# A hand-written instruction order replaced by another: units 8 to 11 moved forward, fewer and finer loads, more placed warm-up matmuls, three scheduled steps pinned

## The chip, the cores and the metric

The kernel runs on one core of a Trainium2 chip. The time is that of one execution on the device in microseconds (us). Engines are named as in the profile: PE (matrix engine), PEld (its weight loads), DVE (vector), ACT (scalar), POOL (GpSimd) and SP, which issues the DMAs.

## The reference, cut to what matters

Two parts follow each other. A decaying recurrence over 4 batches, 8 heads, 768 tokens, head width 32 and state width 16, in chunks of 32 tokens, gives 3072 tokens of 256 numbers. A feed-forward layer with softplus takes them to 2048 and back to 256.

```
log_a = log(clip(a, 1e-6, 1))
for each chunk c:                       # 32 tokens
    cum = cumsum(log_a[c]);  L = causal * exp(cum_i - cum_j)
    y[c]  = (C B^T * L) x  +  (C state) * exp(cum)
    state = exp(sum(log_a[c])) * state + sum_j B_j x_j exp(cum_last - cum_j)
x = y as [3072, 256]
h = x @ w_in;   g = softplus(h);   out = g @ w_out      # [256 -> 2048 -> 256]
```

All values are 32-bit; w_in and w_out arrive as 64-bit numbers. A matmul of full precision in the feed-forward part is made of three fast ones, from a high and a low part of each factor.

## The kernel before, in words

**Units.** The recurrence is cut into 24 units of 128 tokens with all 8 heads; units 0 to 5 are batch 0, and so on. A unit needs: its data (`un`, for units 0 to 3 together with `hc`), a mask of decays built by POOL (`D`), B scaled by decay (`B`) and C scaled by decay (`C`), scores (`S`, PE), the scores times the mask (`M`, two DVE instructions, tile `m`), the new state (`U`, PE and DVE, tiles `zp` and `state`), the previous state spread out (`T`, tile `tb`), the read of the state (`R`, PE) and the sum within the unit (`I`, PE, tile `yp`), the product with the growth factors (`G`, tile `y` on DVE, then `xh` on ACT) and the low part of the result (`X`, tile `xl`). From unit 8 on, units go in pairs: `v` (PE and the states) and `e` (read, state, growth, high and low part).

**Growth factors.** For units 0 to 2 they are made on the chip (`gb`, `gq`). For the others the logs are summed by rows (`growth`), stored to DRAM (`gd`) and read back, spread over 32 partitions per head (`gg`, two loads for 2 or 3 units; the pool holds two such tiles). `loga` and `logr` take the logs of the two layouts of `a`; `ft` and `fr` make the factors by token and by row from them and from the constants `kc` and `kb`.

**Weights.** `w` loads a piece of 64-bit weights (even numbers: w_in, odd: w_out, each for two of the 16 blocks of 128 hidden columns; four raw tiles). `W`, called six times, turns it into a high and a low part: ACT, DVE, DVE, DVE, ACT, DVE.

**Feed-forward steps.** Tokens are cut into six groups of 512 (units 0 to 3 are group 0). `Fj.k` is the first product of group j and block k (six matmuls, tile `hp`), `Hk` the half of `F0.k` for units 0 and 1, `Pj.k` the three steps softplus (ACT, tile `e`), high part (ACT, `gh`) and low part (DVE, `gl`), and `Zj.k` the second product (six matmuls into the accumulators `acc`). Groups 0 and 1 go through blocks 0 to 7 first and through 8 to 15 later; `K`, `L` and `E0` take the accumulators out.

**What sets the order.** Up to `E0` the order of the whole program is the list `ORDER`, word for word, on every engine (`in_order[0]` is True, and each engine is a queue in order). `warmN` places N matmuls without use of their result. From step 28 on a loop over steps takes over: `begin` (F and its parts), `values` (Z), and `fills`: `split_unit`, `attend_scores`, `prefetch`, pairs. There `in_order[0]` is False: PE and the DMAs keep the program's order, while a planner places the work of DVE, ACT and POOL, also between words of `ORDER`. In the profile, what was placed in order has line 127 (L127), the free instructions have their own lines, such as L254, L255, L368 and L384. DMAs have line 137.

Of the kernel before, what the change touches and what calls it, by code (L numbers as in the profile page):

```python
# [50 lines left out]


ORDER = """
zero warm8 la kc kb hc0 w0 loga un0 loga w2 gb hc1 fr0 w4 ft0 fr0 un2 lr hc3 hc2 un6 W0 S0 w6 ft0 W0 un1 W0 un5 D1 B0
un4 W2 un7 fr0 un3 gq0 fr0 D0 W0 ft2 gq0 M0 w5 W0 logr M0 gq2 logr ft2 growth D2 I0 gq2 B2 growth S2 gd G0 U2 W0 G0 S1
M2 W4 X0 fr2 M2 C1 U0 B1 D3 M1 U1 C2 warm3 U0 M1 T1 S3 D4 U1 fr2 U2 T2 R1 S4 B4 T3 B6 W4 W2 R2 C3 B3 I1 W2 W4 C4 I2 G1
gg3 M3 G1 R3 X1 gg10 U3 C5 M3 warm1 M4 I3 D8 U3 M4 fr2 U6 G2 fr2 D7 U4 G3 G2 H0 U6 G3 U4 X2 S7 X3 T4 W2 F0.0 M7 W2 w1
H1 W4 P0.0 R4 W2 P0.0 w3 F0.1 M7 C7 H2 P0.0 D5 P0.1 I4 T7 W6 F0.2 P0.1 un10 W4 H3 W6 P0.2 P0.1 R7 P0.2 W4 F0.3 B7 W1
P0.2 H4 P0.3 G4 I7 W1 G4 B10 P0.3 W6 F0.4 X4 H5 P0.3 P0.4 W1 U7 F0.5 T5 un11 U7 W1 S5 P0.5 T8 w7 W1 W6 S6 M5 W6 w10 W1
R5 W6 W3 Z0.0 M5 W5 W3 D6 I5 W5 P0.4 F0.6 un8 W3 Z0.1 G5 P0.6 W3 gg6 G5 M6 W3 F0.7 w9 X5 P0.6 W3 B8 W7 C8 Z0.2 M6 W7  # L60
D9 G7 I6 W5 G7 P0.5 Z0.3 un9 X7 G6 S11 P0.5 G6 gg8 X6 P0.7 P0.4 F1.0 P0.7 W5 C9 W5 w15 P0.7 S9 P1.0 W5 B9 W9 W7 Z0.4
P0.6 W9 F1.1 W7 P1.0 W9 W7 w8 P1.0 Z0.5 P1.1 W9 W7 W9 w12 F1.2 M9 P1.1 W10 W9 Z0.6 P1.2 P1.1 W8 W10 M9 F1.3 P1.2 W8
D10 W10 Z0.7 P1.3 W8 F1.4 L0 K0 P1.3 W8 Z1.0 P1.3 P1.4 w13 W8 W10 F1.5 W8 W10 w14 P1.2 P1.4 W15 W10 Z1.1 P1.5 P1.4 W13
W15 F1.6 W15 P1.5 W13 P1.5 Z1.2 P1.6 W13 W15 F1.7 W13 P1.6 w11 W15 P1.6 W13 Z1.3 W15 P1.7 W13 W14 F0.8 W12 W14 P1.7
W14 W12 Z1.4 P0.8 P1.7 W12 F0.9 W14 P0.8 W12 W14 P0.8 Z1.5 W12 W14 P0.9 W12 W11 F0.10 P0.9 W11 W11 Z1.6 P0.10 P0.9 W11
F0.11 P0.10 W11 P0.10 Z1.7 W11 P0.11 F0.12 P0.11 K1 P0.11 L1 S8 P0.12 Z0.8 M8 M8 F0.13 P0.12 D11 P0.12 Z0.9 P0.13
F0.14 P0.13 P0.13 Z0.10 P0.14 F0.15 P0.14 P0.14 Z0.11 P0.15 F1.8 P0.15 P0.15 Z0.12 P1.8 v8 P1.8 P1.8 Z0.13 M11 un13
C10 v8 un12 S10 M11 e8 e8 M10 Z0.14 e8 M10 e8 gg12 F1.9 C11 e8 v10 P1.9 P1.9 P1.9 F1.10 v10 e10 P1.10 F1.11 e10 e10
P1.10 e10 P1.10 Z0.15 P1.11 e10 P1.11 P1.11 E0
"""  # L70
# [31 lines left out]


@with_exitstack
def recurrence_then_ffn(ctx: ExitStack, tc: tile.TileContext, fst, un, at, al, w_in, w_out, const, outT):
# [29 lines left out]
    def load(out, in_):  # L135

        tc.keep_in_program_order(nc.sync.dma_start(out, in_))  # L137
# [107 lines left out]
    def split_unit(i):  # L245
        if i < FIRST:
            return
        t = bc_s[i]
        b_rows = p2.tile([P, NQ, P], F32R, tag="b_rows", name=f"b_rows{i}")

        def split(out, j):
            raw = t[:, j * NQ * P : (j + 1) * NQ * P].rearrange("p (q t) -> p q t", q=NQ)
# [1 line left out]
            A.activation(out, raw, AF.Copy, scale=be)  # L254
            V.scalar_tensor_tensor(out, raw, g, out.bitcast(F32), op0=ALU.mult, op1=ALU.add)  # L255
# [678 lines left out]
```

## Time and profile before

| | |
|---|---|
| time, 3 runs | 348.7 us median (347.05 to 349.23) |
| the profiled execution | 347.7 us, its span 345.7 us |
| mean granted clock of PE | 0.975 |
| PE busy | 329.7 us, 95% of the span |
| DVE, ACT, POOL busy | 205.2, 170.9, 37.8 us |
| moved by DMA | 34.99 MB |

A row of the timeline reads: start, duration, engine, line, operation, output<-input, shapes, how many were merged, and in brackets the idle time before and what ended it. A row of the table by windows reads: the window and its length, then busy time and number of instructions of PE, PEld, DVE, ACT and POOL (an engine with none is left out), the granted clock of PE, the busy share of the 16 DMA engines, and GB/s. PE's end times are modelled, so the distance from one start to the next says more than the duration.

### The profile page before, as it was taken

What the parts mean: (1) busy time and instruction counts of PE and PEld (TensorE: products, weight loads), DVE (VectorE), ACT (ScalarE), POOL (GpSimd) and SP (SyncE); (2) the same over time, 40 slices, a digit from 0 to 9 for tenths busy, and PEclk for the clock granted to TensorE, in tenths of its full rate; (3) what the DMA queues carried; (4) which work ended last, traced back from release to release, by engine and by line L of the source; (5) the groups of instructions that cost most, each with busy time, mean ns of one, the idle gap of its engine ahead of it and who ended that gap; (6) DMA issues with size and microseconds to landing.
All of it is one profiled execution on the core that took longest, in us unless ns stands there. A gap on an engine that the chain in (4) does not pass through costs nothing.

```text
span 345.7 us, 5174 instructions
## 1 busy us (share of the span) xinstructions
PE 329.7 (95%) x1972; PEld 258.5 (75%) x1972; DVE 205.2 (59%) x358; ACT 170.9 (49%) x309; POOL 37.8 (11%) x32
## 2 busy tenths in 40 slices
PE   8588999999999879999999999999999999999996
PEld 4335877588878557888888878888888888888885
DVE  0985797999952882666673775677575243222222
ACT  3642863778744252454462572465553443454451
POOL 1432104020010110110110110110110000000000
PEclk9896799999999989999999999999999999999999
DMA  7972547545000504623512514513420100010001
GB/s 241 396 298 70 158 149 248 161 124 174 0 2 0 183 33 124 210 56 128 154 30 93 137 55 145 151 33 111 134 91 12 21 0 2 1 61 2 0 0 61
DMA packets 21895, 34.99 MB, mean 101 GB/s; under 512 B 1648, under 2 KB 11120, under 8 KB 21872
## 3 DMA queue, kind: packets, MB, share of 16 engines
q1 hardware_dynamic: 21872, 34.68, 31.8%
q8 instruction: 15, 0.25, 0.3%
q14 instruction: 8, 0.07, 0.1%
HBM read 28.29 MB, written 3.24 MB: 91 GB/s over the span
## 4 chain that ended last, share of the span: by engine, by line
PE 69%; DMA 13%; DVE 9%; ACT 4%; issue 2%; SPq 2%; ACTq 0%; DVEq 0%
PE acc L127 33%; PE hp L127 31%; DMA gg<-gd 4%; DMA bc<-in_un 3%; DMA gd<-lr 3%; PE yp L127 3%; PE sp L127 2%; DVE w L127 2%; SPq L137 2%; DMA wraw<-in_w_in 1%; DMA un<-in_un 1%; DVE m L127 1%; DMA un<-in_fst 1%; DVE gl L127 1%; ACT e L666 1%
## 5 line engine op out<-in xcount | busy, mean ns | idle before, releaser
L678 DVE TENSOR_TENSOR gl<-e,gh 128x512 fp32r<-128x512 f32 x68 | 54.1, 799 | 52.3 <-ACT gh L672 52.0
L127 PE MATMUL hp<-xh,wih 128*128 128x512 f32 (+1 forms) x204 | 79.1, 388 | 0.3 <-ACT xh L127 0.3
L127 PE MATMUL hp<-xh,wil 128*128 128x512 f32 (+1 forms) x204 | 78.1, 383 | 0.0
L127 PE MATMUL hp<-xl,wih 128*128 128x512 f32 (+1 forms) x204 | 78.1, 383 | 0.0
L127 PE MATMUL acc<-gh,woh 128*128 128x512 f32 x188 | 75.7, 402 | 1.0 <-DVE half L127 0.8
L666 ACT ACTIVATE e<-hp 128x512 f32<-128x512 f32 x68 | 40.5, 595 | 68.6 <-PE hp L127 68.3
L127 PE MATMUL acc<-gl,woh 128*128 128x512 f32 x188 | 73.7, 392 | 0.0
L127 PE MATMUL acc<-gh,wol 128*128 128x512 f32 x188 | 73.6, 391 | 0.0
L127 PEld LDWEIGHTS hp<-xh,wih 128*128 128x128 f32 x204 | 39.2, 192 | 10.5 <-issue 2.3
L672 ACT CAST gh<-e 128x512 fp32r<-128x512 f32 x68 | 42.0, 618 | 6.6 <-PE acc L127 5.0
L127 PEld LDWEIGHTS hp<-xl,wih 128*128 128x128 f32 x204 | 39.4, 193 | 7.3 <-DVE xl L127 0.3
L127 PEld LDWEIGHTS hp<-xh,wil 128*128 128x128 f32 x204 | 39.3, 193 | 7.2
L127 PEld LDWEIGHTS acc<-gh,woh 128*128 128x128 f32 x188 | 35.7, 190 | 10.2 <-ACT e L666 1.8
L127 PEld LDWEIGHTS acc<-gh,wol 128*128 128x128 f32 x188 | 35.4, 189 | 7.9 <-DVE wol L127 0.2
L127 PEld LDWEIGHTS acc<-gl,woh 128*128 128x128 f32 x188 | 35.7, 190 | 6.5 <-DVE gl L678 0.2
L353 POOL TENSOR_SCALAR_AFFINE_SELECT rm<-fc 128x1024 f32<-128x1024 f32 x12 | 18.1, 1510 | 135.0 <-DVE m L412 117.2
L127 DVE TENSOR_TENSOR gl<-e,gh 128x512 fp32r<-128x512 f32 x28 | 19.8, 709 | 14.6 <-ACT gh L127 14.5
L254 ACT ACTIVATE c_all<-bc,kb 128x512 fp32r<-128x512 f32 x12 | 8.7, 724 | 38.2 <-DMA bc<-in_un 38.1
L127 POOL TENSOR_SCALAR_AFFINE_SELECT rm<-fc 128x1024 f32<-128x1024 f32 x12 | 18.2, 1518 | 81.5 <-DVE m L127 74.3
L127 DVE SCALAR_TENSOR_TENSOR w<-wraw,w 128x512 int32<-128x512 int32 x32 | 23.5, 753 | 0.1
L127 ACT CAST gh<-e 128x512 fp32r<-128x512 f32 x28 | 17.4, 621 | 11.3 <-PE acc L127 11.1
L127 ACT ACTIVATE e<-hp 128x512 f32<-128x512 f32 x28 | 16.7, 596 | 10.8 <-PE hp L127 10.4
(93 smaller groups left out, 303.5 us busy)
## 6 DMA issues: line engine op xcount, KB each, us to landing
bc<-in_un SPq DMA_DIRECT2D x12, 512.0 KB
un<-in_fst SPq DMA_DIRECT2D x8, 576.0 KB
wraw<-in_w_in SPq DMA_DIRECT2D x8, 512.0 KB
wraw<-in_w_out SPq DMA_DIRECT2D x8, 512.0 KB
un<-in_un SPq DMA_DIRECT2D x12, 256.0 KB
c_rows<-c_all SPq DMA_DIRECT2D x24, 128.0 KB
gg<-gd SPq DMA_DIRECT2D x18, 128.0 KB
out_t<-o SPq DMA_DIRECT2D x9, 256.0 KB
```

Source lines behind the costliest of these rows:

```text
L127: return lambda *a, **k: tc.keep_in_program_order(f(*a, **k))
L137: tc.keep_in_program_order(nc.sync.dma_start(out, in_))
L254: A.activation(out, raw, AF.Copy, scale=be)
L353: Pl.affine_select(out=rm.rearrange("p h c i -> p (h c) i"), in_=fc[:, u].rearrange("p h c -> p (h c)").unsqueeze(2).broadcast_to([P, NH * ...
L666: A.activation(e, h, AF.Softplus)
L672: A.copy(gh, e)
L678: V.tensor_tensor(gl, e, gh.bitcast(F32), op=ALU.subtract)
```

## The change

Both lists hold the same work except that the number of `warm` matmuls goes from 12 to 30. In the new list, units 4 to 11, the loads and the pieces of weights stand at other places; `un12` and `un13` stand ahead of `Z0.8`. The two layouts of `a` come by one load, and so do the two parts of the constants, each pair into one tile. A `gg` load for a unit below 8 (`gg3`, `gg6`) is made of eight loads, one for each head, in place of two. `in_order[0]` stays True for steps 28, 29 and 30.

```diff
 ORDER = """
-zero warm8 la kc kb hc0 w0 loga un0 loga w2 gb hc1 fr0 w4 ft0 fr0 un2 lr hc3 hc2 un6 W0 S0 w6 ft0 W0 un1 W0 un5 D1 B0
-un4 W2 un7 fr0 un3 gq0 fr0 D0 W0 ft2 gq0 M0 w5 W0 logr M0 gq2 logr ft2 growth D2 I0 gq2 B2 growth S2 gd G0 U2 W0 G0 S1
-M2 W4 X0 fr2 M2 C1 U0 B1 D3 M1 U1 C2 warm3 U0 M1 T1 S3 D4 U1 fr2 U2 T2 R1 S4 B4 T3 B6 W4 W2 R2 C3 B3 I1 W2 W4 C4 I2 G1
-gg3 M3 G1 R3 X1 gg10 U3 C5 M3 warm1 M4 I3 D8 U3 M4 fr2 U6 G2 fr2 D7 U4 G3 G2 H0 U6 G3 U4 X2 S7 X3 T4 W2 F0.0 M7 W2 w1
...
-F0.11 P0.10 W11 P0.10 Z1.7 W11 P0.11 F0.12 P0.11 K1 P0.11 L1 S8 P0.12 Z0.8 M8 M8 F0.13 P0.12 D11 P0.12 Z0.9 P0.13
-F0.14 P0.13 P0.13 Z0.10 P0.14 F0.15 P0.14 P0.14 Z0.11 P0.15 F1.8 P0.15 P0.15 Z0.12 P1.8 v8 P1.8 P1.8 Z0.13 M11 un13
-C10 v8 un12 S10 M11 e8 e8 M10 Z0.14 e8 M10 e8 gg12 F1.9 C11 e8 v10 P1.9 P1.9 P1.9 F1.10 v10 e10 P1.10 F1.11 e10 e10
-P1.10 e10 P1.10 Z0.15 P1.11 e10 P1.11 P1.11 E0
+zero la warm11 kc un2 hc1 hc0 hc2 un0 logr loga un1 logr loga w2 growth gb hc3 ft0 growth un3 gq0 ft0 w1 B2 D0 un5 fr0
+gq0 gq2 fr0 D1 w0 S0 gq2 w7 B0 S1 M0 un6 B1 M0 U0 fr0 M1 D2 I0 fr0 U0 gd M1 C1 S2 T1 un4 D3 W2 G0 un7 U1 C2 M2 U2 R1
+B3 G0 W2 ft2 M2 C3 X0 D5 U1 W1 W2 U3 ft2 I1 fr2 warm3 U2 T2 fr2 S5 G1 T3 G1 U3 W2 R2 T4 S3 W2 w3 M5 X1 M5 I2 gg3 W2 R3
+D4 M3 fr2 W0 warm6 B4 C4 M3 fr2 U4 C5 W0 warm1 D7 S4 G2 U4 gg6 W0 G2 I3 T5 S6 W0 M4 W0 R5 X2 R4 M4 C7 I5 w4 W0 D6 I4
+G3 un11 W3 G5 warm2 W1 G3 un10 H0 G5 W3 warm6 X5 M6 G4 H1 W1 G4 gg8 X3 S7 X4 M6 W1 F0.0 D11 M7 I6 W1 w6 B10 P0.0 F0.1
+W1 P0.0 H2 G6 P0.1 M7 warm1 W4 S10 P0.0 P0.1 D8 W4 G6 Z0.0 P0.1 H3 W4 Z0.1 X6 W4 B6 F0.2 W3 W4 w5 B7 U6 W4 P0.2 F0.3
...
+W13 W9 P1.6 W15 Z1.4 W9 P1.7 W15 W9 P1.7 F0.8 W15 W9 W15 Z1.5 W9 P1.7 P0.8 W9 W15 F0.9 P0.8 W15 W14 P0.8 v8 P0.9 W14
+P0.9 W14 P0.9 Z1.6 W14 M10 W14 C10 F0.10 v8 W14 M10 e8 P0.10 F0.11 e8 P0.10 C11 e8 Z1.7 P0.10 P0.11 gg10 e8 F0.12 e8
+P0.11 K1 S11 P0.11 L1 un13 P0.12 un12 Z0.8 M11 M11 F0.13 P0.12 P0.12 v10 P0.13 F0.14 v10 e10 P0.14 Z0.9 e10 e10 e10
+F0.15 P0.14 e10 P0.14 Z0.10 P0.15 F1.8 P0.15 P0.15 Z0.11 P1.8 F1.9 P0.13 P0.13 Z0.12 P1.9 F1.10 P1.9 P1.9 Z0.13 P1.10
+P1.8 F1.11 P1.8 P1.10 P1.10 Z0.14 P1.11 P1.11 Z0.15 P1.11 E0
 """
+PINNED = 31
...
-    la = cp.tile([P, NB * NU * NH], F32, name="la")
-    lr = cp.tile([P, S * NB * NH // P], F32, name="lr")
+    both_logs = cp.tile([P, 2 * NA], F32, name="both_logs")
+    la, lr = both_logs[:, :NA], both_logs[:, NA:]
...
-    kc = cp.tile([P, K_END], F32, tag="kc", name="kc")
-    kb = cp.tile([P, C_END], F32, name="kb")
+    kept = cp.tile([P, K_END + C_END], F32, name="kept")
+    kc, kb = kept[:, :K_END], kept[:, K_END:]
...
         for g in range(2):
-            src = gd[b, g * 4 : g * 4 + 4, u * P : (u + n) * P].unsqueeze(1).broadcast_to([4, D, n * P])
-            load(gg[:, g, :], src)
+            at = slice(u * P, (u + n) * P)
+            if i < EARLY:
+                for h in range(4):
+                    load(gg[h * D : h * D + D, g, :], gd[b, g * 4 + h, at].unsqueeze(0).broadcast_to([D, n * P]))
+                continue
+            load(gg[:, g, :], gd[b, g * 4 : g * 4 + 4, at].unsqueeze(1).broadcast_to([4, D, n * P]))
...
-        "la": lambda: load(la, at),
-        "kc": lambda: load(kc, const[:, :K_END]),
-        "kb": lambda: load(kb, const[:, K_END:]),
-        "lr": lambda: load(lr, al),
+        "la": lambda: load(both_logs, alr),
+        "kc": lambda: load(kept, const),
...
-    in_order[0] = False
     fills = defaultdict(list)
...
     for s in range(AHEAD, len(steps) + LAG):
+        if s == PINNED:
+            in_order[0] = False
         if begins(*steps[s - LAG]):
```

The tile of `C` for even units from 12 on (`c_all`) lay where `kc` had been; it lies now in the first part of `kept`.

More of the change, by code (lines that the diff above doesn't have):

```diff
@@ L53 @@
 ORDER = """
-zero warm8 la kc kb hc0 w0 loga un0 loga w2 gb hc1 fr0 w4 ft0 fr0 un2 lr hc3 hc2 un6 W0 S0 w6 ft0 W0 un1 W0 un5 D1 B0
-un4 W2 un7 fr0 un3 gq0 fr0 D0 W0 ft2 gq0 M0 w5 W0 logr M0 gq2 logr ft2 growth D2 I0 gq2 B2 growth S2 gd G0 U2 W0 G0 S1
-M2 W4 X0 fr2 M2 C1 U0 B1 D3 M1 U1 C2 warm3 U0 M1 T1 S3 D4 U1 fr2 U2 T2 R1 S4 B4 T3 B6 W4 W2 R2 C3 B3 I1 W2 W4 C4 I2 G1
-gg3 M3 G1 R3 X1 gg10 U3 C5 M3 warm1 M4 I3 D8 U3 M4 fr2 U6 G2 fr2 D7 U4 G3 G2 H0 U6 G3 U4 X2 S7 X3 T4 W2 F0.0 M7 W2 w1
-H1 W4 P0.0 R4 W2 P0.0 w3 F0.1 M7 C7 H2 P0.0 D5 P0.1 I4 T7 W6 F0.2 P0.1 un10 W4 H3 W6 P0.2 P0.1 R7 P0.2 W4 F0.3 B7 W1
@@ L59 @@
[L59 to L63, printed above, removed]
@@ L64 @@
-W15 F1.6 W15 P1.5 W13 P1.5 Z1.2 P1.6 W13 W15 F1.7 W13 P1.6 w11 W15 P1.6 W13 Z1.3 W15 P1.7 W13 W14 F0.8 W12 W14 P1.7
-W14 W12 Z1.4 P0.8 P1.7 W12 F0.9 W14 P0.8 W12 W14 P0.8 Z1.5 W12 W14 P0.9 W12 W11 F0.10 P0.9 W11 W11 Z1.6 P0.10 P0.9 W11
-F0.11 P0.10 W11 P0.10 Z1.7 W11 P0.11 F0.12 P0.11 K1 P0.11 L1 S8 P0.12 Z0.8 M8 M8 F0.13 P0.12 D11 P0.12 Z0.9 P0.13
-F0.14 P0.13 P0.13 Z0.10 P0.14 F0.15 P0.14 P0.14 Z0.11 P0.15 F1.8 P0.15 P0.15 Z0.12 P1.8 v8 P1.8 P1.8 Z0.13 M11 un13
-C10 v8 un12 S10 M11 e8 e8 M10 Z0.14 e8 M10 e8 gg12 F1.9 C11 e8 v10 P1.9 P1.9 P1.9 F1.10 v10 e10 P1.10 F1.11 e10 e10
@@ new lines @@
+G3 un11 W3 G5 warm2 W1 G3 un10 H0 G5 W3 warm6 X5 M6 G4 H1 W1 G4 gg8 X3 S7 X4 M6 W1 F0.0 D11 M7 I6 W1 w6 B10 P0.0 F0.1
+W1 P0.0 H2 G6 P0.1 M7 warm1 W4 S10 P0.0 P0.1 D8 W4 G6 Z0.0 P0.1 H3 W4 Z0.1 X6 W4 B6 F0.2 W3 W4 w5 B7 U6 W4 P0.2 F0.3
+un8 U6 W3 W6 H4 T7 P0.3 w12 W6 U7 W3 R7 W6 P0.2 F0.4 U7 P0.3 W3 I7 P0.4 P0.2 W5 B8 un9 H5 G7 P0.4 P0.3 gg12 Z0.2 G7 W6
+X7 W6 w8 P0.4 F0.5 W5 Z0.3 W6 P0.5 W5 W7 B9 F0.6 C8 P0.5 W5 C9 T8 W5 w10 S8 P0.5 P0.6 W5 P0.6 F0.7 W7 W8 M8 W7 Z0.4 M8
+P0.7 W7 P0.7 D9 F1.0 P0.6 W7 w11 Z0.5 P1.0 W7 P1.0 P0.7 F1.1 W10 W8 P1.0 W10 Z0.6 W8 P1.1 W10 P1.1 F1.2 W8 P1.1 W8 w9
@@ new lines @@
+W10 Z0.7 P1.2 W8 w13 W10 P1.2 F1.3 W10 L0 K0 W12 S9 P1.2 W11 W12 P1.3 W11 Z1.0 W12 P1.3 M9 W12 F1.4 M9 W12 w15 P1.3
+Z1.1 D10 P1.4 W12 P1.4 F1.5 P1.4 W13 Z1.2 W11 P1.5 W13 W11 P1.5 F1.6 W13 W11 w14 P1.5 Z1.3 W13 P1.6 W11 W13 F1.7 P1.6
+W13 W9 P1.6 W15 Z1.4 W9 P1.7 W15 W9 P1.7 F0.8 W15 W9 W15 Z1.5 W9 P1.7 P0.8 W9 W15 F0.9 P0.8 W15 W14 P0.8 v8 P0.9 W14
+P0.9 W14 P0.9 Z1.6 W14 M10 W14 C10 F0.10 v8 W14 M10 e8 P0.10 F0.11 e8 P0.10 C11 e8 Z1.7 P0.10 P0.11 gg10 e8 F0.12 e8
+P0.11 K1 S11 P0.11 L1 un13 P0.12 un12 Z0.8 M11 M11 F0.13 P0.12 P0.12 v10 P0.13 F0.14 v10 e10 P0.14 Z0.9 e10 e10 e10
@@ L104, in recurrence_then_ffn @@
 @with_exitstack
-def recurrence_then_ffn(ctx: ExitStack, tc: tile.TileContext, fst, un, at, al, w_in, w_out, const, outT):
+def recurrence_then_ffn(ctx: ExitStack, tc: tile.TileContext, fst, un, alr, w_in, w_out, const, outT):
     nc = tc.nc
@@ L137, in load @@
         tc.keep_in_program_order(nc.sync.dma_start(out, in_))
-    la = cp.tile([P, NB * NU * NH], F32, name="la")
-    lr = cp.tile([P, S * NB * NH // P], F32, name="lr")
+    NA = NB * NU * NH
+    both_logs = cp.tile([P, 2 * NA], F32, name="both_logs")
+    la, lr = both_logs[:, :NA], both_logs[:, NA:]
     cum = cp.tile([P, S * NB * NH // P], F32, name="cum")
-    kc = cp.tile([P, K_END], F32, tag="kc", name="kc")
-    kb = cp.tile([P, C_END], F32, name="kb")
+    kept = cp.tile([P, K_END + C_END], F32, name="kept")
+    kc, kb = kept[:, :K_END], kept[:, K_END:]
     wih = cp.tile([P, 2, DFF], F32R, name="wih")
@@ L255, in split @@
             V.scalar_tensor_tensor(out, raw, g, out.bitcast(F32), op0=ALU.mult, op1=ALU.add)
-        pool, tag = (p2, "c_all") if i % 2 else (cp, "kc")
-        c_all = pool.tile([P, NQ, P], F32R, tag=tag, name=f"c_all{i}", bufs=1)
+        if i % 2:
+            c_all = p2.tile([P, NQ, P], F32R, tag="c_all", name=f"c_all{i}", bufs=1)
+        else:
+            c_all = kept[:, : NQ * P].bitcast(F32R).rearrange("p (q t) -> p q t", q=NQ)
         split(c_all, 1)
@@ L917 @@
         "un": c(un[FIRST:]),
-        "at": c(a.reshape(NB, NH, NU, P).transpose(3, 0, 2, 1).reshape(P, NB * NU * NH)),
-        "al": c(a.reshape(P, S * NB * NH // P)),
+        "alr": c(
+            np.concatenate(
+                [
+                    a.reshape(NB, NH, NU, P).transpose(3, 0, 2, 1).reshape(P, NB * NU * NH),
+                    a.reshape(P, S * NB * NH // P),
+                ],
+                1,
+            )
+        ),
         "w_in": c(inputs["moe_w_in"]).view(np.int64),
```

## The prediction

> **What bounds the kernel now.** I read the busy times on the page first, then the table by windows, cut where PE changes its behaviour, then the timeline in the bad windows.
>
> ```profile
> PE 329.7 (95%) x1972; PEld 258.5 (75%) x1972; DVE 205.2 (59%) x358; ACT 170.9 (49%) x309; POOL 37.8 (11%) x32
> ```
> ```profile
> 12.00:24.00 12.00, 10.16 (x98) 4.71 (x101) 11.10 (x26) 5.30 (x16) 4.10 (x3) 0.86 1.01 388
> 24.00:36.00 12.00, 9.13 (x70) 4.64 (x62) 7.86 (x19) 4.49 (x17) 2.57 (x2) 0.68 0.17 58
> 62.00:112.00 50.00, 49.76 (x236) 39.10 (x240) 38.36 (x66) 32.38 (x57) 3.83 (x2) 1.00 0.23 69
> 112.00:134.00 22.00, 17.69 (x137) 12.79 (x130) 16.52 (x31) 8.29 (x14) 2.57 (x2) 0.92 0.26 85
> 134.00:345.70 211.70, 208.44 (x1205) 172.29 (x1203) 105.86 (x169) 97.99 (x165) 15.55 (x10) 1.00 0.25 74
> ```
> ```profile
> 66.81 1.36 PE hp L127 x6
> 68.17 1.36 PE acc L127 x6
> ```
>
> PE is the bound, busy 95%, but busy is a modelled end. The chain of waits gives the real pace: six matmuls, one F or one Z, in 1.36 us, 0.227 each. From 62 to 112 us and from 134 us on PE keeps that pace. Nothing in the change lowers its work, so the time can only come from the two other stretches: the **ramp** before 62 us, with a clock of 0.68 and a busy DVE, and the **gap** from 112 to 134 us.
>
> The gap, by tile, in the order hp, acc, sp, yp, zp:
>
> ```profile
> 112.00:134.00 22.00, 7.18 (x24) 4.80 (x24) 2.38 (x4) 0.92 0.26 85
> 112.00:134.00 22.00, 6.13 (x21) 4.47 (x22) 1.28 (x2) 0.00 (x0) 0.92 0.26 85
> 112.00:134.00 22.00, 1.13 (x4) 0.30 (x4) 2.73 (x4) 0.92 0.26 85
> 112.00:134.00 22.00, 4.83 (x80) 3.46 (x72) 1.38 (x2) 0.92 0.26 85
> 112.00:134.00 22.00, 0.32 (x8) 0.16 (x8) 0.81 (x3) 0.92 0.26 85
> ```
>
> 45 large matmuls are 10.2 us, the others at most 1.1, 3.5 (64 of about 0.03, 16 of 0.11) and 0.3: 15.0 us of work in 22. **7 us are lost there.** The timeline says to what:
>
> ```profile
> 113.75 0.34 SPq L137 DMA_DIRECT2D bc<-in_un  x1
> 117.84 0.72 ACT L254 ACTIVATE c_all<-bc,kb 128x512 fp32r<-128x512 f32 x1 [5.50 <-DMA bc<-in_un]
> 122.07 0.59 ACT L127 ACTIVATE e<-hp 128x512 f32<-128x512 f32 x1
> 122.25 0.74 DVE L255 SCALAR_TENSOR_TENSOR c_all<-bc,kb,c_all 128x512 fp32r<-128x512 f32 x1
> 122.91 1.40 DVE L255 SCALAR_TENSOR_TENSOR b_rows<-bc,kb,b_rows 128x512 fp32r<-128x512 f32 x2
> 126.22 0.71 PE L127 MATMUL yp<-cc,tb 128*128 128x128 f32 x4 [2.42 <-DVE tb L127]
> 128.10 0.63 PE L127 MATMUL hp<-xl,wih 128*128 128x512 f32 x1
> 133.45 0.47 PE L127 MATMUL acc<-gh,woh 128*128 128x512 f32 x1 [0.81 <-DVE half L127]
> ```
>
> L254 and L255 are free instructions of units 12 and 13 (`split_unit`) that stand between words of `ORDER`. ACT holds one for 5.50 us, until bc lands, 4.1 us after its issue; the softplus queued behind it comes at 122.07. DVE does c_all and b_rows ahead of the state and tb of unit 11, on which PE waits 2.42 us; after that the clock is at half for a while (0.63 us a matmul).
>
> The ramp:
>
> ```profile
> 4.84 0.30 PE L127 MATMUL sums<-kc,la 128*96 128x5 f32 x2 [0.33 <-DMA kc<-in_const]
> 7.69 0.68 ACT L127 ACTIVATE w<-wraw 128x512 f32<-128x512 f32 x1 [3.29 <-DMA wraw<-in_w_in]
> 8.27 0.87 ACT L127 ACTIVATE fc<-fp 128x384 f32<-128x384 f32 x1
> 9.21 2.77 POOL L127 TENSOR_SCALAR_AFFINE_SELECT rm<-fc 128x1024 f32<-128x1024 f32 x2 [7.04 <-ACT ft L127]
> 12.43 0.68 DVE L127 TENSOR_TENSOR m<-sp,rm 128x512 f32<-128x512 f32 x1
> 24.41 0.29 DVE L127 TENSOR_TENSOR bp<-head_in_h,ft 128x128 f32<-128x128 f32 x1 [1.18 <-DMA head_in_h<-in_fst]
> 33.23 0.43 DVE L127 TENSOR_TENSOR y<-yp,gg 128x256 f32<-128x256 f32 x1 [3.74 <-DMA gg<-gd]
> 33.71 2.07 PE L127 MATMUL sp<-un 64*128 64x512 f32 x2 [0.68 <-DVE y L127]
> 50.22 0.47 PE L127 MATMUL acc<-gh,woh 128*128 128x512 f32 x1
> ```
> ```profile
> 16.09 9.88 DMA gd<-lr
> 26.73 6.37 DMA gg<-gd
> ```
>
> The chain of waits runs here through the growth store and its reload (9.88 and 6.37 us), which end in the 3.74 us that DVE stands at y of unit 3. PE then runs cold: 2.07 us for two records of sp. Z0.0 starts at 50.22.
>
> **The change part by part.** DVE is the busy engine of the ramp, and its instructions overlap a little, so I price them by the distance of starts:
>
> ```profile
> 47.30 0.42 DVE L127 TENSOR_TENSOR tb<-state,kb 128x256 f32<-128x256 f32 x1
> 47.63 0.27 DVE L127 SCALAR_TENSOR_TENSOR state<-state,fr,zp 128x64 f32<-128x64 f32 x1
> 47.83 0.68 DVE L127 SCALAR_TENSOR_TENSOR w<-wraw,w 128x512 int32<-128x512 int32 x1
> 48.43 0.42 DVE L127 TENSOR_TENSOR tb<-state,kb 128x256 f32<-128x256 f32 x1
> ```
>
> 0.60 for one of 512 columns, 0.33 for 256, 0.20 for a small one, 0.36 (estimate between these) for the first integer step of W; logs, growth and the row factors together 2.7.
>
> *The order up to Z0.0.* Counted ahead of the first Z0.0, before: 32 x 0.60 + 17 x 0.33 + 15 x 0.20 + 5 x 0.36 + 2.7 = 32.3 us of DVE, and 28.1 us of PE at full clock by 1.36 per F or Z, half of it per H, and the small matmuls as above. After: 26 x 0.60 + 18 x 0.33 + 11 x 0.20 + 5 x 0.36 + 2.7 = 28.2 us of DVE and 23.9 of PE. So before, Z0.0 came 17.9 us later than DVE's work alone (50.2 - 32.3). Call that overhead O. After, PE reaches the same 28.1 us of work 4.2 us beyond its Z0.0, at 28.2 + 4.2 + O. The gain of the ramp is 50.2 - 32.4 - O = **17.8 - O**. What goes from O:
> - Start. In the old list the first W stands ahead of the factors on ACT and ahead of m on DVE, and waits for its weights until 7.69; m comes at 12.43 with 2.2 us of DVE work behind it: 10.2 of overhead. In the new list no W stands there. The larger loads come later by their additional 96 and 100 KB, together 0.5 us at 388 GB/s, so the first matmul on them goes from 4.84 to 5.3, or to 5.8, where eleven warm matmuls by 0.44 end; with 1.3 for the ten matmuls of the factors and 1.2 on ACT it is 8.3, with 1.4 for POOL's mask 9.7, and m comes at 9.9 with 2.9 us of work behind it: 7.0. That is -3.2.
> - The wait of 1.18 for unit 3's data: `un3` is the eleventh load in place of the twentieth. -1.2.
> - The wait of 3.74 for gg. The store gd has 1.70 MB less ahead of it in the queues (one weight piece, units 4 and 7, which SP now issues behind it): 4.4 us at 388 GB/s, so it lands near 21.6. The eight loads then take SP from 0.34 us (bc, above) to 0.64 (gg, below) each, and the last lands at most 2.9 us after its issue (la, whole by 2.87, below) or 6.4 (gg): 26.9 to 32.5. I take 27.5, near la's end, since each of the eight writes one plain run of partitions as la does. DVE needs it at about 20 (its work ahead of that y) + O so far, near 30. -3.7; with the late end -1.2.
>
> ```profile
> 2.87 0.26 DVE L127 TENSOR_SCALAR la<-la 128x192 f32<-128x192 f32 x1 [2.87 <-DMA la<-in_at]
> 0.98 3.53 PE L127 MATMUL warm<-some 128*32 128x512 bf16 x8 [0.98 <-POOL some L127]
> 19.06 0.81 PE L127 MATMUL warm<-some 128*32 128x512 bf16 x3
> 25.99 2.55 SPq L137 DMA_DIRECT2D gg<-gd  x4
> ```
>
> While gg was under way (24 to 36 us) only 0.17 of the 16 DMA engines was busy. [...]
>
> - Added: 18 warm matmuls, 0.27 (19.06) to 0.44 (0.98) each: 4.9 to 7.9 us on PE's queue ahead of everything behind them. PE would hold 24 us of work and some 10 of warm matmuls in the first 40 us, so part of them stands in the way of the masks' and states' chain. Hidden: nothing lost; without cover: all 7.9. I give back half of the 8.1 gained, 4.
>
> O = 17.9 - 8.1 + 4 = 13.8, and the ramp gains **4** (0 to 8).
>
> *Merged loads* otherwise save two SP issues of some 0.3 us; SP is not waited for there. *The sixteen loads for gg3 and gg6* add 12 issues, up to 7.7 us of SP's time; w4, un11 and un10 stand behind them and are used 8 us later or more, so 0.
>
> *The tail of the list.* Units 8 to 11 and the loads of units 12 and 13 move ahead. `un13` and `un12` had three F and two Z left behind them, and now have seven F and eight Z, 20 us by 1.36; bc takes 4.1. gg10 is loaded later than before, behind the y of units 8 and 9; PE has 10 us of work from there to the y of unit 10, and the load takes 6.4 and 1.3 of issue (2 x 0.64).
>
> *Pinning* keeps the L254 and L255 of units 12 and 13 behind the last word of `ORDER`; of ACT's and DVE's work in steps 28 to 30 nothing is due for another four steps of 2.7 us. The wait of 0.81 for the accumulator and a little remain: the gap falls from 7 to 1, a gain of **6** (4 to 7).
>
> The sum against the profiled execution: 347.7 - 4 - 6 = 337.7; the median of the runs is 1.0 above it: **338.7 us**.
>
> **The rivals.**
> - *Only the gap closes* (ramp 0): the front stays as late because the warm matmuls give back all. Against it: the waits named above have their own causes. 348.7 - 6 = 342.7, between 341.5 and 346.5.
> - *Nothing in sum.* The change does not do what it says: ACT's and DVE's order holds, but the wait moves to gg10 (7.7 against 10 of cover) or to unit 12. 346.5 to 352.
> - *Slower: the front turns PE-bound and cold.* 28.1 us of work and 30 warm matmuls by 0.22 are 34.7 at full clock. At the clock c of the first 50 us that is 34.7/c, plus some 5 of start. With c = 0.62, below the 0.68 of the row, it is 61 against 50.2: 10.8 lost, 6 gained, 353.5. It decides below c = 0.68 over the whole front; for it speaks only that the row's 12 us ran there, against it that the new matmuls stand in the idle places. [...]
> - *More* (ramp 8, gap 7): 333 or less.
>
> **How the numbers follow.** Forecast (334 to 341.5) 0.50, only the gap 0.20, nothing in sum 0.10, slower 0.12, more 0.08. A measurement of this kernel can tell about 1%, 3.5 us, from no change. Faster: 0.50 + 0.08 + 0.15 of the second = 0.73; same 0.05 + 0.10 = 0.15; slower 0.12. The range of 333 to 350 leaves out most of the last two.
>
> **What would show it.** Right: m near 10 us, no wait of DVE for gg at unit 3, the first acc matmul near 42 us, ACT's first L254 without a wait for bc, PE at 1.36 per six between 100 and 130 us. Wrong: a first acc later than 48 us, a granted clock under 0.7 in the first 40 us, or a DVE wait for gg late in the list.

## The result and the profile after

The changed kernel takes **337.44 us** (median of 4 runs, 336.96 to 338.82), the kernel before 348.72 in the same comparison. The ratio is **0.9691, 95% interval 0.9647 to 0.9735**. The forecast was 338.7, the range 333 to 350. The profiled execution after took 336.96 us with a span of 335.0 (before 347.7 and 345.7).

The page of the kernel after, busy time of the engines, and the clock granted to PE in 40 slices:

```profile
PE 326.9 (98%) x1990; PEld 256.8 (77%) x1990; DVE 205.6 (61%) x359; ACT 170.9 (51%) x309; POOL 38.0 (11%) x32
PEclk9999999999999999999999999999999999999999
```

The busy times are those of before within 3 us, in a span that is 10.7 us shorter: no work went away, PE's waits did. The same windows as in the prediction, kernel after (what stands in them has moved forward by up to 11 us):

```profile
12.00:24.00 12.00, 11.95 (x122) 6.68 (x114) 12.00 (x28) 7.37 (x25) 5.42 (x4) 1.00 1.03 382
24.00:36.00 12.00, 11.71 (x115) 6.99 (x116) 11.17 (x24) 5.61 (x16) 4.63 (x3) 1.00 0.52 174
36.00:62.00 26.00, 24.41 (x152) 18.16 (x151) 22.69 (x45) 17.32 (x31) 3.88 (x2) 1.00 0.55 175
62.00:112.00 50.00, 49.60 (x299) 38.87 (x299) 41.28 (x73) 29.00 (x50) 4.56 (x3) 1.00 0.28 89
112.00:134.00 22.00, 21.03 (x93) 16.86 (x93) 10.09 (x19) 12.04 (x20) 1.15 (x1) 1.00 0.27 82
```

From 24 to 36 us the clock is 1.00 in place of 0.68, DVE is busy 11.17 us in place of 7.86, and the DMA engines 0.52 in place of 0.17. From 112 to 134 us PE is busy 21.03 in place of 17.69. The timeline of the ramp after:

```profile
10.20 0.68 DVE L128 TENSOR_TENSOR m<-sp,rm 128x512 f32<-128x512 f32 x1
11.02 0.34 SPq L138 DMA_DIRECT2D gd<-both_logs  x1
20.88 9.39 SPq L138 DMA_DIRECT2D gg<-gd  x16
29.01 0.74 DVE L128 TENSOR_TENSOR y<-yp,gg 128x256 f32<-128x256 f32 x2
30.89 0.88 SPq L138 DMA_DIRECT2D un<-in_fst  x2
37.62 0.29 DVE L128 TENSOR_TENSOR bp<-un,ft 128x128 f32<-128x128 f32 x1 [2.45 <-DMA un<-in_fst]
38.79 0.51 PE L128 MATMUL acc<-gh,woh 128*128 128x512 f32 x1
40.09 0.50 PE L128 MATMUL acc<-gl,woh 128*128 128x512 f32 x1 [0.80 <-DVE gl L128]
50.30 0.29 DVE L128 TENSOR_TENSOR bp<-un,ft 128x128 f32<-128x128 f32 x1 [1.57 <-DMA un<-in_fst]
```
```profile
26.74 1.66 DMA gg<-gd
31.38 6.21 DMA un<-in_fst
```

(The second fence is the chain of waits: start, length, transfer.) The y of unit 3 has no bracket: nobody waits for the growths. In its place stand two new brackets, 2.45 and 1.57 us for the data of units 10 and 8. Unit 10's load was issued with unit 11's from 30.89 on, behind sixteen gg issues that held SP for 9.39 us; unit 8's stands further down the list and was issued at 44.63. The end of the list, after, and the store of `E0` in both kernels (after, before):

```profile
99.95 0.29 DVE L392 TENSOR_TENSOR cc<-un,fr 128x128 f32<-128x128 f32 x1 [2.59 <-DMA un<-in_un]
122.22 0.94 SPq L138 DMA_DIRECT2D out_t<-half  x2
122.34 0.47 PE L128 MATMUL acc<-gh,woh 128*128 128x512 f32 x1 [0.83 <-DVE half L128]
124.58 0.72 ACT L128 ACTIVATE kept<-bc,kept 128x512 fp32r<-128x512 f32 x1
```
```profile
133.33 0.94 SPq L137 DMA_DIRECT2D out_t<-half  x2
```

ACT's first `split` instruction stands behind `E0` and waits for nothing, where L254 waited 5.50 us. `E0` is 11.1 us earlier (133.33 - 122.22); what follows takes 212.8 us (335.0 - 122.22), before 212.4. **So all of the gain was made ahead of `E0`.**

To split it I took, from each trace, the distance of every PE instruction to the next, less the usual distance of its kind. The sum is the time that PE lost; warm matmuls count wholly as lost, the usual distance of a kind is the same for all kernels, and its choice makes the sum uncertain by some 1 us. Before: 23.4 us from 0 to 65 us (the ramp) and 7.8 from 65 to 135 (the gap). After: 17.4 and 3.2. The ramp gave **6.0 us**, the gap **4.6**.

### The profile page after: what moved, and what is told of

Same layout as the page of the kernel before. It is cut to its first block, busy times and chain, and to the rows that moved or that the text cites. A ratio compares the mean times of both kernels' runs of the same rounds, so it can differ in the third digit from the quotient of the medians.

```text
span 335.0 us, 5230 instructions
## 1 busy us (share of the span) xinstructions
PE 326.9 (98%) x1990; PEld 256.8 (77%) x1990; DVE 205.6 (61%) x359; ACT 170.9 (51%) x309; POOL 38.0 (11%) x32
## 4 chain that ended last, share of the span: by engine, by line
PE 84%; DMA 7%; DVE 5%; issue 1%; ACT 1%; POOL 1%; SPq 1%; DVEq 0%; ACTq 0%; POOLq 0%
PE acc L128 37%; PE hp L128 36%; PE yp L128 4%; DMA un<-in_fst 4%; PE sp L128 2%; DMA wraw<-in_w_out 2%; DMA un<-in_un 1%; PE warm L128 1%; DVE m L128 1%; PE end L128 1%; PE zp L128 1%; POOL rm L128 1%; DVE w L128 1%; SPq L138 1%; DMA gg<-gd 0%
## 5 line engine op out<-in xcount | busy, mean ns | idle before, releaser
L686 DVE TENSOR_TENSOR gl<-e,gh 128x512 fp32r<-128x512 f32 x65 | 50.8, 786 | 49.6 <-ACT gh L680 48.8
L128 PE MATMUL hp<-xh,wih 128*128 128x512 f32 (+1 forms) x204 | 78.0, 382 | 0.0
L128 PE MATMUL hp<-xh,wil 128*128 128x512 f32 (+1 forms) x204 | 76.9, 377 | 0.5 <-DVE wil L128 0.5
L128 PE MATMUL hp<-xl,wih 128*128 128x512 f32 (+1 forms) x204 | 76.8, 377 | 0.0
L128 PEld LDWEIGHTS hp<-xh,wih 128*128 128x128 f32 x204 | 38.3, 188 | 10.2 <-issue 2.3
L128 PEld LDWEIGHTS hp<-xh,wil 128*128 128x128 f32 x204 | 38.3, 188 | 8.0 <-DVE wil L128 0.9
L128 PEld LDWEIGHTS hp<-xl,wih 128*128 128x128 f32 x204 | 38.4, 188 | 7.1
L128 DVE TENSOR_TENSOR gl<-e,gh 128x512 fp32r<-128x512 f32 x31 | 21.2, 684 | 14.0 <-ACT gh L128 14.0
L128 DVE SCALAR_TENSOR_TENSOR w<-wraw,w 128x512 int32<-128x512 int32 x32 | 22.7, 725 | 0.1
L128 DVE TENSOR_TENSOR m<-sp,rm 128x512 f32<-128x512 f32 x26 | 17.5, 679 | 0.0
```

The source lines that it names most:

```text
L128: return lambda *a, **k: tc.keep_in_program_order(f(*a, **k))
L686: V.tensor_tensor(gl, e, gh.bitcast(F32), op=ALU.subtract)
```

## The experiments

Theory: the gain is made of two separate repairs, the growth store early enough (ramp) and an undisturbed end of the list (gap). Rivals: the order as a whole does it; the clock does it, by the warm matmuls; or one of the smaller parts (loads by head, merged loads). "Ramp" and "gap" are PE's lost time as above.

| kernel | time, us | ratio to before, 95% interval | ramp | gap |
|---|---|---|---|---|
| before | 348.7 | 1 | 23.4 | 7.8 |
| after | 337.4 | 0.9691 (0.9647 to 0.9735) | 17.4 | 3.2 |
| new list, not pinned | 337.4 | 0.9714 (0.9669 to 0.9760) | 17.5 | 3.9 |
| old list, pinned | 343.7 | 0.9869 (0.9836 to 0.9902) | 24.4 | 2.3 |
| new list, two loads per gg | 336.3 | 0.9670 (0.9633 to 0.9707) | 15.7 | 3.1 |
| new list, warm11 only | 338.1 | 0.9710 (0.9660 to 0.9760) | 17.8 | 3.5 |
| old list, gg by head | 345.2 | 0.9927 (0.9897 to 0.9957) | 21.7 | 6.2 |
| old list, early store | 342.7 | 0.9874 (0.9836 to 0.9912) | 19.9 | 6.3 |
| new list, pinned to step 35 | 342.2 | 0.9844 (0.9806 to 0.9883) | 17.4 | 2.6 |
| new list, loads moved | 335.6 | 0.9670 (0.9635 to 0.9704) | 15.9 | 3.4 |
| the last, not pinned | 336.3 | 0.9700 (0.9658 to 0.9742) | 16.0 | 4.1 |
| new list, four loads | 339.6 | 0.9786 (0.9746 to 0.9826) | 18.8 | 3.0 |
| old list, early store and pin | 340.0 | 0.9807 (0.9732 to 0.9882) | 22.4 | 2.4 |
| the same and six warm | 340.2 | 0.9780 (0.9743 to 0.9817) | 22.0 | 2.5 |

The kernel before ran beside each group, at 347.3 to 348.7 us; the ratios compare best.

**Is the pin needed?** The new list with `PINNED = 28`, that is, with the planner free from step 28 on as before:

```diff
-PINNED = 31
+PINNED = 28
```

> The new list, with steps 28 to 30 free again (the old place of the switch). Theory 'loads': the gap closed because the data of units 12 and 13 are loaded 20 us ahead of the list's end; then this stays at 336 to 339, and the first ACT instruction on bc waits little. Theory 'pin': free instructions of units 12 and 13 again come between the list's words and hold ACT and DVE; then 340 to 344, with a PE loss of 3 to 6 us between 95 and 125 us. By the prediction both count, and I expect 339 to 341.

Timeline of the new list, not pinned:

```profile
100.00 0.29 DVE L392 TENSOR_TENSOR cc<-un,fr 128x128 f32<-128x128 f32 x1 [2.60 <-DMA un<-in_un]
101.30 0.72 ACT L260 ACTIVATE c_all<-bc,kept 128x512 fp32r<-128x512 f32 x1 [2.32 <-DMA bc<-in_un]
```

It takes 337.4 us, as much as the kernel after. The planner does put `split` between the list's words again, at 101.30, but its load stands earlier in the list, so ACT waits 2.32 us in place of 5.50, and PE loses 3.9 us there in place of 7.8. So the new list closes most of the gap without the pin; I had expected 339 to 341 us. That the earlier loads do it is read from this trace; no run moved them alone.

**And in the old list?** The old list with steps 28 to 30 pinned:

```diff
-    in_order[0] = False
     fills = defaultdict(list)
...
     for s in range(AHEAD, len(steps) + LAG):
+        if s == 31:
+            in_order[0] = False
```

> The old list with steps 28 to 30 pinned, nothing else. Theory 'pin': the stall in the gap goes, 342 to 344 against 348.7 before. Theory 'loads': bc still lands near 118 us, and what waits for it only moves behind the list's end, 346 to 349.

Windows of this kernel, and DVE's wait for gg (in total, times, longest):

```profile
24.00:36.00 12.00, 9.71 (x81) 5.48 (x69) 7.12 (x18) 3.99 (x16) 2.57 (x2) 0.62 0.20 66
112.00:134.00 22.00, 21.17 (x176) 16.13 (x175) 15.45 (x29) 8.62 (x15) 2.57 (x2) 1.00 0.32 109
```
```profile
DVE y L127 <- DMA gg<-gd: 4.5, 2, 4.0
```

It takes 343.7, 4.7 us less than before in that comparison (348.4). PE is busy 21.17 of 22 us in the gap (17.69 before); the ramp is untouched, with its clock of 0.62 and its wait for gg. So the pin in the old list and the new list without the pin each repair most of the same 7 us, and neither needs the other.

**The loads by head.** The new list, each growth tile by two loads of four heads again:

```diff
-            if i < EARLY:
+            if i < 0:
```

> The new kernel with gg3 and gg6 by two loads each again. Theory 'early store': the reload is in time because the store of the growths goes earlier; with two loads gg lands near 28 us, as y of unit 3 needs it (29), SP is free 7 us sooner, and the wait of 2.45 us for unit 10's data goes: 336 to 338.5. Rival 'by head': the finer loads are what removed the wait; it comes back with 2 to 4 us, 339.5 to 342.

Timeline of this kernel, SP and DVE:

```profile
21.03 2.38 SPq L138 DMA_DIRECT2D gg<-gd  x4
28.91 0.82 SPq L138 DMA_DIRECT2D un<-in_fst  x2
36.26 0.29 DVE L128 TENSOR_TENSOR bp<-un,ft 128x128 f32<-128x128 f32 x1 [1.17 <-DMA un<-in_fst]
48.63 0.29 DVE L128 TENSOR_TENSOR bp<-un,ft 128x128 f32<-128x128 f32 x1 [1.25 <-DMA un<-in_fst]
```

It takes 336.3 us, and no y waits for gg with the slow form either: with the store issued at 11 to 12 us, either form lands in time. The loads by head cost SP 9.39 us in place of 2.38, and the waits of units 10 and 8 shrink from 2.45 and 1.57 to 1.17 and 1.25. Of the 7 us that SP is free sooner only 2.0 reach unit 10's load (28.91 in place of 30.89), because the weights' load ahead of it goes out at 26.95, 3.5 us after the last gg. The step is not needed here; whether it costs the 1 us that stands between the medians is not separated.

The other way round, the **old list with its late store**, gg3 and gg6 by head:

```diff
+            at = slice(u * P, (u + n) * P)
+            if i < EARLY:
+                for h in range(4):
+                    load(gg[h * D : h * D + D, g, :], gd[b, g * 4 + h, at].unsqueeze(0).broadcast_to([D, n * P]))
+                continue
```

> The old kernel with gg3 and gg6 by eight loads each, nothing else. The store still lands near 26 us. Theory 'by head removes the wait': the eight loads take 0.3 to 0.6 us each and land at once, y of unit 3 comes at 30 to 31 instead of 33.2, and the time falls by 1 to 3 us, to 345.5 to 347.5. Theory 'early store': the loads begin too late for it to matter, the wait stays over 2 us, 347.5 to 349.

Timeline of this kernel, the first y of each of the two tiles:

```profile
32.90 0.42 DVE L127 TENSOR_TENSOR y<-yp,gg 128x256 f32<-128x256 f32 x1 [1.89 <-PE sp L127]
57.98 0.42 DVE L127 TENSOR_TENSOR y<-yp,gg 128x256 f32<-128x256 f32 x1 [0.51 <-DMA gg<-gd]
```

It takes 345.2 us, ratio 0.9927. DVE's wait of 3.74 us for the growths of unit 3 is gone although the store's place in the list is the old one; DVE now waits there for PE, and 0.51 us for the second tile. The first y of that tile starts 5.4 us after the first issue (27.51 to 32.90), where it started 7.2 us after it before (25.99 to 33.23). So the finer loads do land sooner after their issue, as the prediction had it; they are worth that only where the store is late. The chains of waits have 1.66 us for a load by head in the kernel after, against 6.37 for one of four heads before; the load by head moves only a quarter of the data, and what makes it shorter is not shown.

**The store.** The old list, with the logs by row loaded right behind `la`, `logr` and `growth` made behind `gb`, and `gd` issued behind unit 1's load:

```diff
-zero warm8 la kc kb ...
+zero warm8 la lr kc kb hc0 w0 loga un0 loga w2 gb logr logr growth growth hc1 ... W0 un1 gd W0 ...
```

> The old kernel with the row layout of the logs loaded second, the growths computed right behind the first logs, and their store issued behind un1, ahead of units 5, 4, 7 and 3; all else as before. By the prediction's third item the store lands near 20 us, gg by 28, the wait of 3.74 us at y of unit 3 goes, and as the ramp's chain ran through it, the time falls by 2 to 4 us: 344.5 to 346.5. Rival: another wait takes its place at once (the weights, or unit 3's data, which now land later), 347.5 to 349.5.

Timeline and windows of this kernel:

```profile
11.78 0.33 SPq L137 DMA_DIRECT2D gd<-lr  x1
19.11 4.36 SPq L137 DMA_DIRECT2D gg<-gd  x4
```
```profile
24.00:36.00 12.00, 9.76 (x136) 7.35 (x134) 10.33 (x23) 7.10 (x21) 3.20 (x3) 1.00 0.30 105
112.00:134.00 22.00, 17.46 (x115) 13.37 (x114) 13.89 (x23) 9.73 (x16) 2.37 (x2) 1.00 0.39 124
```

It takes 342.7 us, 5.1 less than before in that comparison (347.8). DVE no longer waits for the growths of unit 3. PE's loss falls by 3.5 us in the ramp and by 1.5 in the gap, which no edit of this run touched and which stays bad (17.46 busy of 22). So this is the ramp's repair in the main.

**Do the two add up?** The old list with the early store and the pin, the edits of two runs above together:

```diff
-zero warm8 la kc kb ...
+zero warm8 la lr kc kb hc0 w0 loga un0 loga w2 gb logr logr growth growth hc1 ... W0 un1 gd W0 ...
...
+        if s == 31:
+            in_order[0] = False
```

> The old list with two edits: the growth store early (logs by row loaded and made ahead, the store behind unit 1's load) and steps 28 to 30 pinned. Theory 'two repairs': the new list gains through two separate things, the early store (5 to 6 us by the run with it alone) and an undisturbed tail (4.7 us by the run with the pin alone), which stand in different stretches and add up: 337 to 339.5 us against 348 before, within 2 us of the new list, the first growth load waited for by nobody, and PE without a long idle time between 100 and 130 us. Rival 'the order itself': what is left of the new list (units 8 to 11 sooner, fewer W ahead, more warm matmuls) is worth as much again, and this one stays at 341 or more. Third: early store and pin get in each other's way (the tail comes earlier, so the data of units 12 and 13 are late again): 341 to 343 with a wait for unit data in ORDER's last words.

It takes 340.0, ratio 0.9807, between the two forecasts. The gap closes (2.4). The product of the two single ratios is 0.9745, inside the interval, but the median gains 7.3 of the 9.8 us. The timelines of PE (first the run with the early store alone, then this one) and this one's windows show something that went wrong here, in a stretch where both have the same list:

```profile
27.11 0.68 PE L127 MATMUL yp<-cc,tb 128*128 128x128 f32 x4 [1.82 <-DVE y L127]
```
```profile
27.86 0.68 PE L127 MATMUL yp<-cc,tb 128*128 128x128 f32 x4 [2.50 <-DVE y L127]
```
```profile
30.00:32.00 2.00, 2.00 (x23) 1.72 (x24) 2.00 (x7) 0.96 (x3) 1.90 (x2) 0.50 0.15 50
32.00:34.00 2.00, 2.00 (x7) 0.83 (x6) 1.57 (x4) 0.40 (x1) 0.04 (x1) 0.50 0.03 8
34.00:36.00 2.00, 2.00 (x8) 1.44 (x7) 0.86 (x2) 1.51 (x2) 0.00 (x0) 0.50 0.52 101
```

PE stood 2.50 us, behind a y that waited on DVE for the data of unit 3, where it had stood 1.82, and then ran at half clock for three windows. In the ramp it lost 22.4 us in place of 19.9. To see whether that was the missing 2.5 us, **six warm matmuls** were put into the wait:

```diff
-gg3 M3 G1 R3 X1 ...
+gg3 M3 warm6 G1 R3 X1 ...
```

> The old list with the early store, the pin, and six warm matmuls ahead of the read of unit 3, where PE stood 2.50 us and the clock then fell to 0.50 for some 5 us in the run without them. Theory 'clock': what that run (340.0) lacked was the clock; with the granted clock at 1.00 from 24 to 36 us the time is 337 to 338.5, within 1 us of the new list, and the DVE wait for unit 3's data (1.47) stays. Rival 'the order itself': the clock holds and the time stays at 339.5 to 341, since the later work waits for DVE anyway. Third: the clock falls in spite of the six, and nothing changes.

Windows and DVE's waits of this kernel:

```profile
24.00:36.00 12.00, 10.58 (x127) 7.70 (x126) 10.77 (x25) 6.20 (x19) 2.56 (x2) 1.00 0.31 92
```
```profile
26.06 0.29 DVE L127 TENSOR_TENSOR bp<-head_in_h,ft 128x128 f32<-128x128 f32 x1 [1.23 <-DMA head_in_h<-in_fst]
55.34 0.29 DVE L127 TENSOR_TENSOR bp<-un,ft 128x128 f32<-128x128 f32 x1 [1.60 <-DMA un<-in_fst]
58.49 0.43 DVE L127 TENSOR_TENSOR y<-yp,gg 128x256 f32<-128x256 f32 x1 [1.72 <-DMA gg<-gd]
```

The clock is 1.00 and the time is the same, 340.2 (0.9743 to 0.9817, clear of the kernel after). The theory that the clock was missing falls: DVE still stands 1.60 us for unit data (2.25 at 56.87 without the six), and now 1.72 us for growths on top. A difference under 1 us could not be seen here, since the four runs without the six lie between 338.72 and 343.04.

What is left to the new list as an order is some 3 us (0.978 against 0.969); it lies in the ramp (22.0 against 17.4). These waits need not be what it is, since removing such waits from the new list gave PE nothing (loads moved, below). The trace points to the start, where the old list has its first W ahead of the factors:

```profile
10.04 0.43 DVE L127 TENSOR_SCALAR w<-w 128x512 int32<-128x512 int32 x1 [4.21 <-ACT w L127]
14.06 1.27 DVE L127 TENSOR_TENSOR m<-sp,rm 128x512 f32<-128x512 f32 x2
```

DVE stands 4.21 us at that W, and m comes at 14.06 in place of 10.20. That this is the 3 us is argued, not shown: no run moved the first W alone.

**The warm matmuls of the new list.** All but `warm11` left out:

```diff
-... U3 ft2 I1 fr2 warm3 U2 T2 ... D4 M3 fr2 W0 warm6 B4 C4 M3 fr2 U4 C5 W0 warm1 D7 ...
+... U3 ft2 I1 fr2 U2 T2 ... D4 M3 fr2 W0 B4 C4 M3 fr2 U4 C5 W0 D7 ...
```

> The new list without the 19 warm matmuls after the first eleven. Theory 'clock': without them PE's granted clock falls under 0.9 somewhere between 12 and 36 us and the time rises to 339 to 344. Theory 'in the way': they cost PE's queue up to 5 us in the ramp, and the time falls to 333 to 336.5. Theory 'no matter': PE is busy enough without them and waits for DVE where they stood: 336.5 to 338.5.

Windows of this kernel:

```profile
25.00:30.00 5.00, 5.00 (x60) 2.83 (x52) 4.50 (x9) 2.48 (x7) 1.87 (x2) 0.68 0.21 63
35.00:40.00 5.00, 2.90 (x14) 1.30 (x12) 2.04 (x6) 4.16 (x7) 0.71 (x1) 0.85 0.93 305
```

The clock falls to 0.68 and 0.85 in these windows (0.990 over the whole execution), in place of 1.00 all through the kernel after, and the time goes from 337.4 to 338.1, not separated (0.9710 against 0.9691). Some 7 us at half clock (an estimate: 337.2 us at a mean of 0.990, if all of the loss is at 0.50) cost nothing that can be told here, and neither do the warm matmuls that avoid them.

**More pinning.** The free `cc` of step 31 still waits between the list's words, so five more steps were pinned:

```diff
-PINNED = 31
+PINNED = 36
```

> The new kernel with steps 28 to 35 pinned in place of 28 to 30. In the new kernel free instructions of unit 13 still stand between the list's words (a cc at 100 us waits 2.59 us for its data on DVE, with M10 and the state behind it). If those waits cost PE its 0.9 us between 100 and 105 us, the time falls by 0.5 to 1.5: 336 to 337. If PE's queue covers them, 337 to 338; if pinned work of later steps now holds ACT or DVE in front of something due, 338 to 341.

Timeline of this kernel:

```profile
140.14 0.72 ACT L260 ACTIVATE c_all<-bc,kept 128x512 fp32r<-128x512 f32 x1 [1.69 <-DMA bc<-in_un]
140.90 0.75 DVE L261 SCALAR_TENSOR_TENSOR c_all<-bc,kept,c_all 128x512 fp32r<-128x512 f32 x1 [3.79 <-ACT c_all L260]
147.77 1.27 DVE L128 TENSOR_TENSOR o<-acc,half 128x512 f32<-128x512 f32 x2
148.59 0.47 PE L128 MATMUL acc<-gh,woh 128*128 128x512 f32 x1 [3.47 <-DVE o L128]
```

It is slower than any of the three forecasts, 342.2 us. The list's end is no worse (`E0` at 121.59), but in steps 31 to 35 the program's order is a bad one for DVE: `o`, which empties the accumulator, stands behind the splits and scores of later units, DVE is held 3.79 us by ACT, and PE waits 3.47 for `o`. Here the program's order pays up to the end of the list that was written for it, and not beyond.

**Loads moved.** Two loads per gg, `un10` ahead of `un11`, `B8` and `B10` behind `B9`; and then the same without the pin:

```diff
-G3 un11 W3 G5 warm2 W1 G3 un10 ...
+G3 un10 W3 G5 warm2 W1 G3 un11 ...
...
-            if i < EARLY:
+            if i < 0:
```

> The new kernel with gg3 and gg6 by two loads, un10 ahead of un11, and B8 and B10 behind B9, where nothing waits for them yet. The waits of DVE for units 10 and 8 (2.45 and 1.6 us in the new kernel, 1.2 and 1.25 with two loads) go. If DVE's idle time in the ramp passes to the end one to one, as the prediction's sum has it, the time falls from the 336.3 of two loads by 1 to 2.4: 334 to 335.5. Rival: PE then waits for the scores of unit 10 or for the weights, and it stays at 336 to 337.

```diff
-PINNED = 31
+PINNED = 28
```

> The new list with its loads moved (two loads per growth tile, unit 10 ahead of unit 11, two B steps later), and not pinned: the planner is free from step 28 on. Theory 'the pin is not needed where the list is undisturbed': 335.6 to 337, equal to the pinned one (335.6) within its interval. Rival 'pin': 339 or more, with ACT or DVE held by a load of unit 12 or 13 ahead of a softplus of the list.

335.6 and 336.3 us. The waits for the data of units 10 and 8 are gone (DVE's longest between 30 and 60 us is 0.65, for ACT), but PE's loss in the ramp stays at 15.9 (15.7 with two loads alone): the waits were off the path. 335.6 lies between the two forecasts; PE's loss sides with the rival, though PE's longest wait from 30 to 60 us is 0.27 us, for `gl`, and neither for scores nor for weights. 335.6 is the fastest version seen; it isn't separated from the kernel after, nor from its unpinned form.

**Merged loads.** The new kernel with the logs and the constants by two loads each, the second part of the logs behind unit 2's data:

```diff
-zero la warm11 kc un2 hc1 ...
+zero la warm11 kc kb un2 lr hc1 ...
```

> The new kernel with the logs and the constants by two loads each again, the second part of the constants right behind the first and the logs by row behind unit 2's data. Theory 'merging is neutral': 336.5 to 338.5, the first m within 0.5 us of 10.2. Rival 'the merged loads are late': the two layouts of the logs and both parts of the constants come sooner when split, m moves ahead by about 0.5 us or more and the time with it: 336 or less. Other side: two more issues on SP move everything behind them by some 0.6 us, m by as much, and the store of the growths too: 338.5 or more.

Timeline of this kernel:

```profile
6.62 0.26 DVE L128 TENSOR_SCALAR lr<-lr 128x192 f32<-128x192 f32 x1 [6.62 <-DMA lr<-in_alr]
13.29 0.69 DVE L128 TENSOR_TENSOR m<-sp,rm 128x512 f32<-128x512 f32 x1 [0.29 <-PE sp L128]
```

It takes 339.6 us, slower than the kernel after (0.9786 against 0.9691, intervals apart), and m comes at 13.29 in place of 10.20. It is the outcome of the "other side", but for another reason than the two issues: the list has `logr` ahead of `loga` on DVE, and the late `lr` (6.62) holds the logs by token behind it; behind that PE takes 1.97 us for the eight `gp` matmuls at 9.15 us, in place of 1.08 at 6.46 in the kernel after. So the late place of that load costs 2 to 3 us in the new list. PE's lost time shows less of it (18.8 in place of 17.4), as the profiled execution is the fastest of the four. What merging does apart from the place stays open, since no version of the new list had `lr` right behind `la`.

## Why the prediction was right, step by step

- **The bound, and where time can come from: right.** PE's work is unchanged, the steps behind `E0` take 212.8 us in place of 212.4, and all of the gain lies in the ramp and the gap.
- **The start: right.** m at 10.20 (9.9 forecast), with no W ahead of it. A new list whose m comes 3.1 us later (four loads) takes 2.1 us more.
- **The wait for gg: right.** No y waits for gg, and gd is issued at 11.02. I wanted both the early store and the finer loads for it; the store alone is enough. By itself it is worth 5.1 us in the old list, 3.5 of PE's loss in the ramp, where I had 3.7 for the wait. The new list with a late store was not tried.
- **"I give back half of the 8.1 gained, 4": the term that was mis-sized.** The first acc came at 38.79, not near 42, so O is 38.8 - 28.2 = 10.6, not 13.8, near the 9.8 without any give-back. Leaving the added warm matmuls out changed the time by 0.7, not separated from nothing. They stood in PE's idle places. By the sum the ramp should then give 17.8 - 10.6 = 7.2; PE's loss shows 6.0, where I had 4, and the 1.2 between them stays open. O also holds the 2.45 us wait for unit 10, so some 2 us must have gone elsewhere that the sum does not name.
- **"w4, un11 and un10 stand behind them and are used 8 us later or more, so 0": wrong.** The sixteen issues took 9.39 us, unit 10's load landed late, and DVE stood 2.45 us for it; 1.17 of these stay with fewer issues, so about half belongs to them. The 1.57 us for unit 8 hardly do (1.25 stay). With fewer issues the ramp's loss went from 17.4 to 15.7; the medians differ by 1 us, which is not separated.
- **The tail and the pin: the right mechanism, too generous.** I had the gap fall from 7 to 1; it fell from 7.8 to 3.2, a gain of 4.6 in place of 6. What stayed is the wait of 0.83 for `half`, which I had, and a free `cc` of step 31 (2.59 us of DVE at 99.95), which pinning to step 30 doesn't reach. I booked the gain to both edits; either one alone gives most of it.
- **The rivals.** "Only the gap closes" fell with the clock and the gg wait. "Cold and PE-bound" fell with the clock of 1.00. A clock under 0.68 over the whole front, as it asks, was in no run; with 0.68 from 25 to 30 us (warm matmuls left out) the time hardly moved.
- The two sizes missed in opposite directions: 4 + 6 was forecast, 6.0 + 4.6 measured. That the total lies within 1.3 us owes something to that.

## What to carry to other kernels

Look at what an early store-and-reload waits for and issue the store as soon as its input exists: two small edits of the old list (early store, three steps pinned) gave two thirds of what a whole new order gave (ratios 0.9807 and 0.9691). The two remedies for the stall at gg did not add here (new list, loads by head 337.4 us, by four heads 336.3), and DMA issues were queue time as well (sixteen held SP for 9.39 us, four for 2.38; DVE waited 2.45 and 1.17 us for a load behind them): count what stands behind them on the issuing engine, and check its user's date before writing "0". Where DVE and data paced the front, some 7 us of the matrix engine at half clock cost nothing that could be told (338.1 us against 337.4), and extra matmuls in its idle places bought nothing (340.2 against 340.0).

## What the runs showed of the hardware

- The length of a wait of PE alone did not decide the clock. Half clock came some 2 us behind a wait of 2.50 us (0.50 from 30 to 36 us, old list with both edits) and behind one of 2.10 us that ended at 26.39 us in the kernel before (0.50 from 29 to 38 us); it did not come behind one of 1.82 us (old list, early store, clock 1.00 from 24 to 36 us), nor behind one of 3.47 us in the new list pinned to step 35, whose clock is 1.00 throughout.
- The clock mattered less than expected: 0.50 from 30 to 36 us, or 1.00 with six warm matmuls, 340.0 and 340.2 us.
- Sixteen loads of one head took SP 9.39 us, 0.59 each with pauses between them; four of four heads took 2.38, 0.60 each. In the old list by head, ten issues, eight of them of one head, took 4.88 us, 0.49 each. So here an issue for a quarter of the data took nearly as long, 0.49 to 0.59 us against 0.60. Four issues of four heads took 4.36 us in the old list with the early store, and why is open.
